# Batch 2's queries and keys turned by crossbar transposes from SyncE's queue, and two evictions split between VectorE and ScalarE, in a fused retention and expert kernel

## The chip, the cores and the metric

The kernel runs on one core of one Trainium2 chip. The metric is device time in microseconds (us): the median of three runs, 312.85 us before the change (312.38 to 313.4).

The engines by their short names: PE is TensorE (matmuls; PEld its weight loads), DVE is VectorE, ACT is ScalarE, POOL is GpSimd and SP is SyncE, which here only issues transfers. A transfer issued by SP waits in SP's queue, one issued by ScalarE in ScalarE's. "T" or "turn" below means: put a tile's 128 rows on its columns, so that PE can contract over the other dimension.

## What is computed

Retention over 8 batches of 8 heads, 576 positions and 64 dimensions, then a two-layer expert network on its result:

```python
scores = scale * np.matmul(q, k.transpose(0, 1, 3, 2))
Dmat = np.where(rel >= 0, gamma[:, None, None] ** rel[None, :, :], 0.0)
ret = np.matmul(scores * Dmat, v)             # per head; rel = row - column
x = ret.transpose(0, 2, 1, 3).reshape(B * S, H * D)      # 4608 x 512
h = x @ w_in                                             # 4608 x 2048
out = (h * sigmoid(beta * h)) @ w_out                    # 4608 x 512
```

Inputs and output are in f32; the kernel's matmuls take bf16 and add in f32.

## The kernel before

**The work.** Of each batch's 576 positions, 512 make four chunks of 128; the 64 left over (the tails) are taken in pairs of batches. Chunks are numbered through: 0 to 3 are batch 0, 4 to 7 batch 1, 8 to 11 batch 2. Since the decay is a power of the distance, it is put into the queries (`gq`) and the values (`gv`), and what remains is causal attention without softmax. For a chunk, `a_sc` (L312) multiplies turned keys `kT` with turned queries `qT` into scores `sc`, VectorE masks them into `R` (L332), `a_O` (L353) multiplies `R` with the values, `a_cross` (L334) adds what earlier chunks of the batch have left in a state, `a_x` (L370) copies the result out of PSUM into `xT`, and `a_st` (L383) adds the chunk to the state, which ScalarE copies to SBUF (`sbd`, or `end` after the last chunk; L398). The network runs on blocks of 512 rows: `up` (L403) makes one of 16 column groups of `h` and ScalarE applies the gate (L412); `down` (L416) makes one of four row groups of the output in four steps, VectorE copies it out (L430) and SP stores it (L433).

**How queries and keys are prepared.** SP loads them (`load_q` L80, `load_kv` L93). POOL (VectorE for batches 0 and 1) scales the queries into `qs` (L246); POOL casts the keys into `kn` (L272) and scales the values into `vn` (L254). Then they are turned in one of two ways. For batches below `XB = 3`, PE does it: `t_q` (L292) has two groups of eight transposes (L296) into a PSUM tile, copied to `qT` by ScalarE for one group and VectorE for the other (L297); `t_k` (L299) has four (L302), copied to `kT` by ScalarE (L303). From batch 3 on, and for the tails, `turn` (L279) has a crossbar transpose do it, SBUF to SBUF, issued from ScalarE's queue (L280): two for the queries of a batch (`x_q`), one for the keys of two chunks (`x_k`).

**The order.** It is written out by hand. `fill` is the list of network steps in the order in which PE takes them; a step (a unit) is one `up` or a quarter of one row group of a `down`. `d0` is the place where block 0's downs begin, `u1` where block 1's ups begin; `base[1]` is `u1 + 10`. The first twenty ups of block 1 are halves (two chunks of columns each), since its later chunks come late. Steps of the attention, of the loads and of the preparation have a place in `fill` as their due time, and `merged` (L440) puts them out by it, so that each engine's instructions, SP's and ScalarE's queues among them, stand in the order of these due times. An engine takes its instructions in this order; one that waits holds up all behind it.

`pair_steps` (L544) gives the due times of two chunks: `first` (state, scores of both) at `at`, `second` (products with the values, the cross terms, the copies to `xT`) at `to = at + 5`. For batch 2 the first pair's `at` is `lo = base[1] + 11` (L568). The second pair's is `hi`, eight units before block 2 begins.

Batch 1's chunks 4 to 7 have their own list (L530 to L536). Their copies to `xT` are made by ScalarE for even chunks and VectorE for odd ones (L381); chunk 3 alone is split, two pairs of heads on each engine (L378, L379). PE's halves of `up` on block 1 need `xT` of chunks 4 and 5 first, of 6 and 7 ten units later.

A transfer carries one of eight semaphores in turn, and waits for the transfer that had it last, eight issues before.

Of the kernel before, what the change touches and what calls it, by code (L numbers as in the profile page):

```python
# [19 lines left out]
def kernel(  # L20
# [10 lines left out]
    nc = tc.nc  # L31
# [9 lines left out]
    CB = MB // P  # L41
# [25 lines left out]

    NQ = 6
    E = CB
    XB = 3  # L70
    q_tiles, kv_tiles = {}, {}

    def load_q(b):
# [151 lines left out]
    def xt(m):  # L225
        if m not in xts:
            xts[m] = xpool.tile([P, HP, CB, P], BF16, name="xT", tag="xT" if m < B else "xTt", bufs=3 if m < B else 1)
        return xts[m]

    state_ps = {}  # L230
    batch, pair, live = {}, {}, {}
# [44 lines left out]
    def heads(t, p):  # L276
        return t[:, 2 * p:2 * p + 2, :].rearrange("p h d -> p (h d)")

    def turn(dst, src):  # L279
        nc.scalar.dma_start_transpose(dst.rearrange("p j pr s -> p (j pr) s"), src.rearrange("p j h d -> p (j h d)"))  # L280

    def x_q(b, u):
        turn(batch[b]["qT"][:, 2 * u:2 * u + 2], batch[b]["qs"][:, 2 * u:2 * u + 2])

    def x_k(b, u):
        kn, kT = pair[b, u]
        turn(kT, kn)

    def x_tail(i):
        turn(live[i]["qkT"], live[i]["qk"])  # L290

    def t_q(b, u):  # L292
        T = psum.tile([P, CB, 2, P], BF16, name="T", tag="mm" if u else "O", bufs=3 if u else 2)
# [5 lines left out]
    def t_k(i):  # L299
        T = psum.tile([P, HP, P], BF16, name="T", tag="sc" if i in (CB + 2, CB + 3) else "O", bufs=2)  # L300
        for p in range(HP):
            nc.tensor.transpose(T[:, p, :], heads(live[i]["kn"], p), ident[:])  # L302
        nc.scalar.copy(live[i]["kT"], T[:])  # L303

    def q_cols(i, r, p):

# [46 lines left out]
    def a_O(i):  # L353

        b, c = seq[i]
        L = live[i]

        early = i < E
        if not early:
            L["O"] = psum.tile([P, HP, P], F32, name="O", tag="O", bufs=2)  # L360
        O, R, vn = L["O"], L["R"], L["vn"]
        crossed = b is None or c > 0
        for j, p in [(n // HP, n % HP) if early else (n % 2, n // 2) for n in range(H)]:
            nc.tensor.matmul(O[j * D:(j + 1) * D, p, :], vn[:, 2 * p + j, :], R[:, j, p, :],  # L364
                             start=p == 0 and not (early and crossed), stop=early or not crossed,
                             skip_group_check=True)
        if early:
            a_x(i)

    def a_x(i):  # L370
        b, c = seq[i]
        O = live[i]["O"]
        if b is None:
            x = xt(B)[:, :, c, :]
        else:
            x, O = xt(b)[:, :, :, c * PC:(c + 1) * PC], O.rearrange("k p (i s) -> k p i s", i=CB)
        if i == CB - 1:
            nc.vector.tensor_copy(x[:, :2], O[:, :2])  # L378
            nc.scalar.copy(x[:, 2:], O[:, 2:])  # L379
        else:  # L380
            (nc.scalar.copy if i < E or i < 2 * E and i % 2 == 0 else nc.vector.tensor_copy)(x, O[:])  # L381

    def a_st(i):  # L383

# [65 lines left out]
    def F(f, *a):  # L450
        return lambda: f(*a)
# [9 lines left out]
    t_q(0, 1)  # L461
    pre(0)
    t_k(0)
    warm_up(2, 128)
    a_sc(0)
    a_st(0)
    pre(1)
    t_k(1)
    warm_up(1, 128)
    a_cross(0, True)  # L470
    a_O(0)
    a_sc(1)
    a_cross(1, True)
    pre(2, (0,))
    t_k(2)
    a_st(1)
    a_O(1)
# [28 lines left out]
    u1 = len(fill)  # L506
# [3 lines left out]
    base = {1: u1 + 10}  # L510
# [7 lines left out]
    def second(i):  # L518
        for f in (a_O, lambda j: a_cross(j, False), a_x):
            f(i)  # L520
            f(i + 1)
        a_st(i + 1)
# [21 lines left out]
    def pair_steps(i, at, to):  # L544
        b, c = seq[i]
        st = [(at, F(first, i)), (to, F(second, i))]
        if b is None:
            return st + [(at - 31, F(load_tail, c)), (at - 21.5, F(pre, i)), (at - 21, F(load_tail, c + 1)),
                         (at - 13, F(pre, i + 1)), (at - 12, F(x_tail, i)), (at - 9.5, F(x_tail, i + 1))]
        n = full.index(i)  # L550
        if b < XB:
            if c == 0:
                st += [(at - 12 + x, F(pre_q, b, x)) for x in range(4)]
                st += [(at - 5.5, F(t_q, b, 0)), (at - 4.5, F(t_q, b, 1))]
                st += [(at - 6.5 + x / 2, F(pre, i + x)) for x in range(CB)]
            return st + [(at - 3.5, F(t_k, i)), (at - 2.5, F(t_k, i + 1))]
        if c == 0:
            st += [(at - 30, F(load_q, b))] + [(at - 20 + x, F(pre_q, b, x)) for x in range(4)]
            st += [(at - 14 + 1.5 * x, F(x_q, b, x)) for x in range(2)]
        return st + [(at - 28, F(load_kv, n)), (at - 26, F(load_kv, n + 1)), (at - 16, F(pre, i)),  # L560
                     (at - 15, F(pre, i + 1)), (at - 10.5, F(x_k, b, c // 2))]

    todo = list(range(2 * CB, len(seq), 2))
    for n in range(1, B - 1):

        take = [i for i in todo if seq[i][0] == n + 1 or n == B - 2 or seq[i] == (None, 0) and n == CB - 1]
        todo = todo[len(take):]
        lo, hi = (base[n] + 11, base[n + 1] - 8) if n == 1 else (base[n] + 3, base[n + 1] - 8)  # L568
        if len(take) == 2 and n > 1:
            hi -= 6  # L570
        for x, i in enumerate(take):
            at = lo + x * (hi - lo) / (len(take) - 1)
            streams.append(pair_steps(i, at, at + 5))
# [32 lines left out]
```

## Time and profile before

| | |
|---|---|
| median of the runs | 312.85 us (312.38 to 313.4) |
| span of the profiled execution | 310.4 us |
| what lies around the span, against the median | 2.45 us |
| instructions in the span | 5341 |
| PE busy | 299.4 us |
| ScalarE, VectorE, POOL busy | 141.5, 110.1, 96.4 us |
| moved by DMA | 52.79 MB, mean 170 GB/s |
| crossbar transposes | 24, all on ScalarE's queue |
| granted TensorE clock, mean | 1.000 |

The profile is of one execution. Its time in the same measure as the runs is not recorded apart from the span, so the span and the 2.45 us stand for it. Times in views are microseconds from the start of the span. A row of a timeline has the start, the length of the stretch from its first instruction's start to its last one's end, the engine (SPq and ACTq are the issues of transfers), the line, the operation, the tiles as out<-in and the count. A row of the chain has the start, the time that counts towards the end, and what it went to. The time from a transfer's issue to its landing is given apart from these.

### The profile page before, as it was taken

Reading aid. Unit: us, or ns where it says so; the run is one execution under the profiler, and the core shown is the slowest. Engines: PE = TensorE matmul, PEld = TensorE weight load, DVE = VectorE, ACT = ScalarE, POOL = GpSimd, SP = SyncE. Lnnn points to the kernel's source line nnn. Section 1 sums busy time; section 2 is a strip of 40 time slices with the busy share of each in tenths; the row PEclk is TensorE's granted clock in tenths of the full one; section 3 lists DMA queues with packets and bytes.
Section 4 is the critical chain, followed back from the end, with each engine's and each line's share of the span. In section 5 each row is a group of like instructions: output and inputs, shape, how many; then the busy total and the mean of one; then the engine's idle time right before and its main releaser. Section 6 shows DMA issues by size and latency. Waiting matters only on the chain.

```text
span 310.4 us, 5341 instructions
## 1 busy us (share of the span) xinstructions
PE 299.4 (96%) x2142; PEld 157.3 (51%) x2177; DVE 110.1 (35%) x196; ACT 141.5 (46%) x250; POOL 96.4 (31%) x131
## 2 busy tenths in 40 slices
PE   7789999999999999999999999999999999999996
PEld 5544456765454454445544544545455454444444
DVE  6554476342433142434431434133415420010012
ACT  5577626984147502661077106720574037206700
POOL 4663026846524281362228021912420000000000
PEclk9999999999999999999999999999999999999999
DMA  7999999999979989996989598949832110041011
GB/s 202 220 354 386 380 239 269 234 233 200 234 163 170 215 183 230 230 204 98 243 228 112 120 211 224 194 100 208 195 60 50 68 70 0 9 93 37 0 67 71
DMA packets 123897, 52.79 MB, mean 170 GB/s; under 512 B 105680, under 2 KB 116320, under 8 KB 123872
## 3 DMA queue, kind: packets, MB, share of 16 engines
q1 hardware_dynamic: 98496, 46.15, 61.3%
q10 hardware_dynamic: 25376, 6.30, 13.5%
q8 instruction: 17, 0.28, 0.4%
q14 instruction: 8, 0.07, 0.1%
HBM read 36.71 MB, written 9.44 MB: 149 GB/s over the span
## 4 chain that ended last, share of the span: by engine, by line
PE 89%; SPq 4%; DMA 3%; issue 1%; DVE 1%; ACT 0%
PE po L423 40%; PE ph L410 38%; DMA wt<-in_moe_w_in_dram 3%; SPq L93 3%; PE O L364 3%; PE sc L322 3%; PE O L350 2%; PE st L393 2%; SPq L177 1%; PE T L296 1%; PE T L302 1%; DVE xT L381 0%; DVE w_in_sb L185 0%; PE O L347 0%; SPq L80 0%
## 5 line engine op out<-in xcount | busy, mean ns | idle before, releaser
L412 ACT ACTIVATE gT<-ph,beta_sb 128x512 bf16<-128x512 f32 (+1 forms) x154 | 100.4, 659 | 83.1 <-PE ph L410 82.4
L410 PE MATMUL ph<-xT,w_in_sb 128*128 128x512 bf16 (+1 forms) x599 | 128.9, 365 | 2.5 <-DVE w_in_sb L185 1.1
L423 PE MATMUL po<-w_out_sb,gT 128*128 128x512 bf16 (+2 forms) x590 | 127.4, 368 | 1.3 <-issue 0.5
L410 PEld LDWEIGHTS <-w_in_sb 128*128 128x128 bf16 x616 | 58.7, 98 | 64.3 <-DVE w_in_sb L185 2.2
L423 PEld LDWEIGHTS <-gT 128*128 128x128 bf16 x608 | 57.0, 98 | 62.3
L332 DVE TENSOR_TENSOR R<-sc,causal 128x512 bf16<-128x512 f32 x71 | 44.3, 684 | 56.5 <-PE sc L322 55.0
L430 DVE COPY ot<-po 128x512 f32<-128x512 f32 (+2 forms) x38 | 25.0, 662 | 86.2 <-PE po L423 83.4
L254 POOL TENSOR_TENSOR vn<-kvn,gv 128x512 bf16<-128x512 f32 x32 | 33.3, 1042 | 16.8 <-DMA kvn<-in_v_dram 15.5
L272 POOL CAST kn<-kvn 128x512 bf16<-128x512 f32 x32 | 19.6, 612 | 58.9 <-DMA kvn<-in_k_dram 58.5
L246 POOL TENSOR_TENSOR qs<-qn,gq 128x512 bf16<-128x512 f32 x24 | 24.3, 1042 | 27.3 <-DMA qn<-in_q_dram 27.3
L381 DVE CAST xT<-O 128x512 bf16<-128x512 f32 x30 | 19.4, 687 | 34.8 <-PE O L350 15.5
L398 ACT CAST sbd<-st 64x256 bf16<-64x256 f32 x48 | 17.5, 364 | 18.8 <-PE st L393 16.6
L398 ACT CAST end<-st 64x256 bf16<-64x256 f32 x16 | 5.9, 366 | 29.4 <-PE st L393 29.3
L393 PE MATMUL st<-vn,kn 128*128 128x128 bf16 x128 | 12.4, 220 | 0.2 <-POOL vn L254 0.2
L364 PEld LDWEIGHTS <-vn 128*64 128x64 bf16 x288 | 8.7, 110 | 6.7 <-issue 6.1
L364 PE MATMUL O<-R,vn 128*64 128x128 bf16 x288 | 11.9, 223 | 0.0
L303 ACT COPY kT<-T 128x512 bf16<-128x512 bf16 x12 | 6.9, 586 | 8.8 <-PE T L302 7.7
L393 PEld LDWEIGHTS <-kn 128*128 128x128 bf16 x128 | 9.0, 98 | 3.5
L322 PE MATMUL sc<-qT,kT 64*128 64x128 bf16 x256 | 10.3, 218 | 0.4 <-ACT kT L303 0.2
L322 PEld LDWEIGHTS <-kT 64*128 64x128 bf16 x288 | 8.1, 94 | 3.8 <-ACT kT L303 1.5
L350 PE MATMUL O<-qT,sbd 128*128 128x128 bf16 x96 | 8.3, 221 | 0.3 <-ACT xT L381 0.2
L207 PE MATMUL ph<-warm 128*128 128x128 f32 (+1 forms) x24 | 6.9, 426 | 1.2 <-DVE warm L118 1.2
(56 smaller groups left out, 85.8 us busy)
## 6 DMA issues: line engine op xcount, KB each, us to landing
qn<-in_q_dram SPq DMA_DIRECT2D x16, 512.0 KB, 5.5
kvn<-in_k_dram SPq DMA_DIRECT2D x32, 256.0 KB, 5.9
kvn<-in_v_dram SPq DMA_DIRECT2D x32, 256.0 KB, 5.7
out_dram<-ot SPq DMA_DIRECT2D x31, 256.0 KB, 2.8
wt<-in_moe_w_out_dram SPq DMA_DIRECT2D x4, 1024.0 KB, 9.5
wt<-in_moe_w_in_dram SPq DMA_DIRECT2D x4, 512.0 KB, 7.3
wt<-in_moe_w_in_dram SPq DMA_DIRECT2D x2, 1024.0 KB, 11.7
out_dram<-ot SPq DMA_DIRECT2D x9, 128.0 KB, 2.4
```

The lines of the kernel that those rows point to most:

```text
L246: e.tensor_tensor(batch[b]["qs"][:, cs, hs], q_tiles[b][:, hs, cs].rearrange("p h i d -> p i h d"), gq[:, cs, hs].unsqueeze(3).to_broadcas ...
L254: nc.gpsimd.tensor_tensor(live[i]["vn"][:], kv_tiles.pop(i)[:, 1], gains(gv, c), ALU.mult)
L272: nc.gpsimd.tensor_copy(kn[:, c % 2], t[:, 0])
L322: nc.tensor.matmul(view(sc[j][:, p, :]), L["kT"][r, p, :], rhs, start=True, stop=True, skip_group_check=True)
L332: nc.vector.tensor_tensor(R[:, j], sc[j][:], causal4[:] if i == CB - 1 else m_b, ALU.mult)
L364: nc.tensor.matmul(O[j * D:(j + 1) * D, p, :], vn[:, 2 * p + j, :], R[:, j, p, :], start=p == 0 and not (early and crossed), stop=early or ...
L393: nc.tensor.matmul(st[:, p, :], heads(L["kn"], p), heads(L["vn"], p), start=(c == 0 and p == 0), stop=True, skip_group_check=True)
L398: nc.scalar.copy(s[r, :, j * D:(j + 1) * D], st[r, :, j * D:(j + 1) * D])
L410: nc.tensor.matmul(ph, w_in_sb[:, ko, fo * P:(fo + 1) * P], xts[m][:, ko, :, w], start=(ko == 0), stop=(ko == KO - 1))
L412: nc.scalar.activation(gts[m][:, fo, :, w], ph, ACT.Silu, scale=beta_sb[:, fo:fo + 1])
L423: nc.tensor.matmul(po[:, :nn], gT[:, fo, ms, :], w_out_sb[:, fo, n0:n0 + nn], start=(fo == 0), stop=(fo == FO - 1))
L430: nc.vector.tensor_copy(ot, po[:, :nn])
```

## The change

- `XB` becomes 2 and is no longer a bound but one batch, the third (batch 2): its queries and keys are turned by crossbar transposes from SP's queue. Later batches and the tails keep theirs on ScalarE's. `t_q` and `t_k` are left to batches 0 and 1.
- Batch 2's preparation gets due times counted from `u1`; on POOL the order of instructions stays as it was. On SP the transposes of the queries (two) and of the first pair's keys stand behind block 0's four stores and ahead of the loads of batch 3's queries and its first two chunks; that of the second pair's keys stands behind these loads.
- Batch 2's first pair is due at `base[1] + 14` for `base[1] + 11`.
- The copies to `xT` of chunks 5 and 7 are split as chunk 3's is. ScalarE keeps chunks 4 and 6.
- The copy of chunk 7's turned keys goes from ScalarE to VectorE.

```diff
-    XB = 3
+    XB = 2
...
-    def turn(dst, src):
-        nc.scalar.dma_start_transpose(dst.rearrange("p j pr s -> p (j pr) s"), src.rearrange("p j h d -> p (j h d)"))
+    def turn(b, dst, src):
+        (nc.sync if b == XB else nc.scalar).dma_start_transpose(dst.rearrange("p j pr s -> p (j pr) s"), src.rearrange("p j h d -> p (j h d)"))
...
     def x_tail(i):
-        turn(live[i]["qkT"], live[i]["qk"])
+        turn(None, live[i]["qkT"], live[i]["qk"])
...
-        nc.scalar.copy(live[i]["kT"], T[:])
+        (nc.vector.tensor_copy if i == 2 * CB - 1 else nc.scalar.copy)(live[i]["kT"], T[:])
...
-        if i == CB - 1:
+        if i < 2 * CB and i % 2 and i != 1:
             nc.vector.tensor_copy(x[:, :2], O[:, :2])
             nc.scalar.copy(x[:, 2:], O[:, 2:])
         else:
-            (nc.scalar.copy if i < E or i < 2 * E and i % 2 == 0 else nc.vector.tensor_copy)(x, O[:])
+            (nc.scalar.copy if i < E or i < 2 * E else nc.vector.tensor_copy)(x, O[:])
...
-        if b < XB:
+        if b == XB:
             if c == 0:
-                st += [(at - 12 + x, F(pre_q, b, x)) for x in range(4)]
-                st += [(at - 5.5, F(t_q, b, 0)), (at - 4.5, F(t_q, b, 1))]
-                st += [(at - 6.5 + x / 2, F(pre, i + x)) for x in range(CB)]
-            return st + [(at - 3.5, F(t_k, i)), (at - 2.5, F(t_k, i + 1))]
+                st += [(u1 + 2 + x, F(pre_q, b, x)) for x in range(4)]
+                st += [(u1 + 6.5 + x / 2, F(pre, i + x)) for x in range(2)]
+                st += [(u1 + 9.5 + x / 2, F(pre, i + 2 + x)) for x in range(2)]
+                st += [(u1 + 10.1 + x / 10, F(x_q, b, x)) for x in range(2)]
+            return st + [(u1 + (12.1 if c == 0 else 20.1), F(x_k, b, c // 2))]
...
-        lo, hi = (base[n] + 11, base[n + 1] - 8) if n == 1 else (base[n] + 3, base[n + 1] - 8)
+        lo, hi = (base[n] + 14, base[n + 1] - 8) if n == 1 else (base[n] + 3, base[n + 1] - 8)
```

## The prediction

> **What bounds the kernel now.** I read the page's first two parts, then the chain of work that ended last, then the timelines of PE and of SP's queue around 60 to 80 us, where the change falls. From the page (busy time; 40 slices; DMA queues):
>
> ```profile
> PE 299.4 (96%) x2142; PEld 157.3 (51%) x2177; DVE 110.1 (35%) x196; ACT 141.5 (46%) x250; POOL 96.4 (31%) x131
> ...
> DMA  7999999999979989996989598949832110041011
> ...
> q1 hardware_dynamic: 98496, 46.15, 61.3%
> q10 hardware_dynamic: 25376, 6.30, 13.5%
> ```
>
> PE is the bound: what takes a microsecond off PE takes it off the end, and a microsecond in which PE waits is added. The second thing to see is the row of nines under DMA up to slice 11 (85 us): while batch 2 is fetched and prepared, the transfer engines are full. q1 is SP's queue, q10 ScalarE's, which carries the 24 crossbar transposes of later batches.
>
> The chain, in order of time (start us, us, what), around the steps that go:
>
> ```profile
> 62.28 0.45 PE T L296 x8
> ...
> 64.04 0.22 PE T L302 x4
> ...
> 66.32 0.22 PE st L393 x4
> 66.54 0.55 PE sc L322 x16
> ...
> 76.96 0.22 PE T L302 x4
> ...
> 80.22 0.55 PE sc L322 x16
> ```
>
> L296 and L302 are the transposes of queries and keys on PE; the sc at 66.54 belongs to batch 2's first pair of chunks (8 and 9), that at 80.22 to its second (10 and 11).
>
> **What goes.** Two groups of eight query transposes (0.45 us each) and four of four key transposes (0.22 each), all in the chain: 2 x 0.45 + 4 x 0.22 = 1.78 us of PE. Of these 1.34 stand before 66.54 and 0.44 behind it. Their copies out of PSUM go too (ScalarE 1.01 and 4 x 0.59 us, VectorE 0.69), off the path: at most 0.3 us, since PE has gaps of 0.1 to 0.3 us while ScalarE is full from 62 to 66 us.
>
> **What is moved.** The first pair's products are put three units later (base + 14 for base + 11). Each unit is four matmuls of 128x512, 0.865 us by the chain's 4.42 us for 20. That is an exchange of order and costs nothing by itself. Without a wait, the sc of chunks 8 and 9 would come at 66.54 - 1.34 + 2.60 = 67.8 us. It now waits for two query transposes and one key transpose from SP's queue.
>
> **When they land.** In the changed program SP issues in the same order as before up to the last two stores of block 0 (L433); then come the three transposes, then the loads of batch 3 (two of queries, four of keys and values), then the second pair's transpose. So SP reaches them when it now reaches L80. SP's timeline (start, us, what):
>
> ```profile
> 61.00 1.02 SPq L93 DMA_DIRECT2D kvn<-in_v_dram  x1
> 62.12 3.78 SPq L433 DMA_DIRECT2D out_dram<-ot  x2
> 65.95 1.04 SPq L80 DMA_DIRECT2D qn<-in_q_dram  x2
> ```
>
> Those two stores need blocks that VectorE had written by 51.2 us; SP is late because the queue is full, not for want of data, and nothing in the change lightens the queue ahead of them. The operands of the transposes are ready earlier: POOL ends chunk 9's keys at 61.4 us, in an order that is unchanged. So the first transpose is issued at 65.95. What one costs, by two of ScalarE's at 204 us, when the transfer engines were nearly idle (one tile's instructions in a window; duration min/median/max in ns):
>
> ```profile
> L280 ACTq DMA_TRANSPOSE qT<-qs x2: 1249/1274/1298, 204.5 to 205.8; - x2
> DMA to landing us min/median/max: 3.2/3.2/3.2
> ```
>
> No row shows a transpose on SP's queue, so I bound the landing of the third (the keys). Early end: 65.95 + 2 x 1.27 + 3.2 = 71.7. Late end: they stand in line behind the last store (issued 65.07, 4.1 to landing: 69.2), each taking 1.75 us: q10 held 13.5% of 310.4 us for 24. That gives 69.2 + 3 x 1.75 = 74.4. At 1.3 us each, the issue pace, it is 73.1. I take 72.4, between the issue-bound 71.7 and this 73.1, since rows at 117 to 119 us move 224 GB/s with transposes nearly alone, 1.2 us for one.
>
> Advanced Engine Details and Errata, section X-Bar Transpose (TRN2), in the Trainium skill holds transposes to be as fast as plain transfers. Here the queue totals give 150 GB/s against 243 for q1, though in the stretch named they come near. By the page the line would move at q1's 1.08 us for 256 KB, and the keys would land at 72.4 as well.
>
> **The sum.** Products start at 72.5 instead of 67.8: PE idles 4.7 us. Against before the end moves by 72.5 - 66.54 - 2.60 (three units already done) - 0.44 (transposes no longer to come) = **+2.9 us** (bounds +2.2 and +4.9). The break-even landing is 69.5 us. Nothing later gives it back: from 67 us on the chain is PE to the end, with no wait over about 0.6 us.
>
> **PE's clock after the gap.** The longest idle time of PE in this profile is about 0.6 us, so no row shows what 4.7 us do. The trace's clock records give the nearest rows: full clock is granted from 4.9 us, 3.7 us after the first matmul (1.25), and half again at 312.1, 4.8 us after the last one ends (307.35). A drop would cost up to half of such a 3.7 us stretch, 1.85 us; no drop costs 0. The gap is within 0.1 us of the row's 4.8, so I take the middle, **+0.9**.
>
> TensorE: Matmul & The Clock Gate, Part 1, in the Trainium skill says that an idle window of about 3.4 us brings half clock, on a grid that does not start with the kernel; the two records are 90 such windows apart, which agrees. By it 1.7 us would be added for one window, in those executions whose grid lies so.
>
> **The eviction splits and the moved copy.** Chunks 5 and 7 go half by VectorE, half by ScalarE. In the one such split now, the waits list ScalarE's half as waiting for VectorE's (L379 for L378, 0.7 us): they run one after the other, 425 + 372 ns and 34 between, 0.83 us against 0.69 whole. But two of PE's four next matmuls need only the first half, so PE's first group ends some 0.08 us sooner: 0.15 for both places. Chunk 7's key copy goes from ScalarE (0.59) to VectorE, between a half of its 691 ns for 128x1024 and 0.59, in 1.5 us of its idle time. All this lies ahead of 67.8, so the wait swallows it; it counts only if there is no wait.
>
> **Behind the transposes.** The batch 3 loads queue behind them, some 3.3 to 5 us later. Their products start at 91.94 now, keys landed at 87.5: 4.4 us of room, and PE itself is 2.9 later. ScalarE's transposes for batch 3 wait until the second pair's has landed. That one lands at 72.4 + 8.0 (what the six loads took from 69.2 to 77.2) + 1.3 to 1.75 = 81.7 to 82.2; PE asks for it at 80.22 + 2.9 = 83.1. So it is hidden.
>
> Own time: span 310.4 plus 2.45 around it is the median of the runs shown, 312.85. With +2.9 and +0.9: **316.7 us**.
>
> **Rivals.**
> 1. *The transposes land in time* (the other side). Mechanism: SP gets past the stores early, and the 1.78 + 0.15 us come off: **310.9**. It decides from a landing at 69.5, that is SP at the transposes by 69.5 - 5.7 = 63.8 or sooner; fully only at 67.8, SP at 62.1. For it: the stores' bare issue is 0.36 us each and they take 3.78, so a stretch of 3 us could shrink. Against: the same DMAs are ahead, on full engines. 0.12. Partly so, within 0.3%: 0.06.
> 2. *The second pair decides.* If SP's issue behind the first three is stretched (now one load there takes 3.2 us), the second pair's keys land after 83.1, and ScalarE's copies of the state, queued behind its waiting transposes, are late for the product at 85.76 + 2.9. At a landing of 86 the shift is 86 - 80.2 = 5.8: **318.7**. Against: 82 by the sum above. 0.10.
> 3. *The forecast* with its unknowns: 0.72, from 315.0 (71.7, no drop) to 319.6 (74.4 and a drop).
>
> The range, 313.9 to 319.7, holds the forecast's bounds, most of rival 2 and a little of an earlier SP; rival 1 is left out. About 0.3% is what a measurement can tell from no change: slower 0.82, same 0.06, faster 0.12.
>
> **What would show it.** In the changed profile: three L280 on SPq from about 66 us on; in the waits PE's L322 (or its weight load) waiting some 4.7 us for a DMA of kT or qT; an idle PE in slices 9 to 10; perhaps a PEclk digit below 9 after it; no L296 or L302 after 60 us. It would be wrong if SP issues the first transpose before 63.8, or if the keys land within 3 us of a late issue.

## The result, and the profile after

| | before | after |
|---|---|---|
| median of 6 runs each, us | 312.81 (312.38 to 315.01) | **317.38** (314.93 to 319.54) |
| ratio after / before | | **1.0136** [1.0107, 1.0166], slower by 1.4% |
| span of the profiled execution, us | 310.4 | 312.7 |
| that execution's own time, us | | 314.93 |
| mean granted TensorE clock in it | 1.000 | 0.999 |
| crossbar transposes on SP's queue / on ScalarE's | 0 / 24 | 4 / 24 |

The ratios in this document and their intervals are the record's estimates over all runs of a group. They are not the quotients of the medians, which here is 1.0146.

The runs of after are far apart. Each, with the mean clock that PE was granted in it: 314.93 (0.999), 316.17 (0.995), 316.95 (0.995), 317.80 (0.994), 318.21 (0.993), 319.54 (0.988). The profiled execution is the quickest of them, and the only one that kept its clock. So its trace shows the wait alone, and the clock has to be read from other traces below.

From the page of after, the answer to the page of before (busy time; 40 slices of 7.8 us; DMA queues):

```profile
PE 298.2 (95%) x2110; PEld 155.6 (50%) x2145; DVE 109.2 (35%) x196; ACT 138.1 (44%) x246; POOL 96.3 (31%) x131
...
PE   7789999968999999999999999999999999999996
...
PEclk9999999999999999999999999999999999999999
DMA  8999999999999799995998495949943110041012
...
q1 hardware_dynamic: 102720, 47.20, 63.4%
q10 hardware_dynamic: 25376, 6.30, 15.2%
```

PE is still the bound and has a microsecond less to do, but its ninth and tenth slices (62.5 to 78.2 us) are down to 6 and 8 tenths. q1 carries 1.05 MB more, and the DMA row is still full from its second slice to its thirteenth.

SP's timeline of after, answering to the three lines of before (start, us, what):

```profile
60.90 0.94 SPq L93 DMA_DIRECT2D kvn<-in_v_dram  x1
61.94 2.51 SPq L433 DMA_DIRECT2D out_dram<-ot  x2
64.61 3.40 SPq L280 DMA_TRANSPOSE qT<-qs  x2
68.11 1.28 SPq L280 DMA_TRANSPOSE kT<-kn  x1
69.44 1.15 SPq L80 DMA_DIRECT2D qn<-in_q_dram  x2
...
76.78 2.24 SPq L280 DMA_TRANSPOSE kT<-kn  x1
```

The transposes stand behind block 0's last two stores and ahead of batch 3's loads. SP came to them at 64.61; L80, which had this place before, came at 65.95.

The chain that ended last, around the same steps (start, the time that counts, what):

```profile
60.90 5.39 DMA kvn<-in_v_dram
...
67.50 0.50 SPq L280
...
68.11 3.16 DMA kT<-kn
71.27 0.05 issue
71.32 0.62 PE sc L322 x16
...
81.80 0.22 PE st L393 x4
82.02 0.55 PE sc L322 x16
```

L296 and L302 are gone from it. In their place it leaves PE for a load of values, SP's issues of the transposes (the piece at 67.50 is the end of the second query transpose's) and the transfer of the keys. The step from the load to SP is the profile's inference: the queries and keys that are turned here were ready by 61.2 us. The keys land at 71.27, 3.16 us after their issue, and the first pair's scores start 0.05 later. PE's timeline (idle time and its releaser in brackets), and PE's waits (us in total, times, longest):

```profile
67.47 0.39 PE L393 MATMUL st<-vn,kn 128*128 128x128 bf16 x4
71.32 0.62 PE L322 MATMUL sc<-qT,kT 64*128 64x128 bf16 x16 [3.46 <-DMA kT<-kn]
```

```profile
PE sc L322 <- DMA kT<-kn: 3.5, 1, 3.5
```

This is the longest wait in PE's list. Without it the scores would have come at 71.32 - 3.46 = 67.86. Against before PE is 1.80 us late at the second pair's scores (82.02 for 80.22), 1.96 at 107 us and 2.31 from 135 us to its end (309.65 for 307.35). The second pair does not wait: its keys landed at 81.40, 0.62 us before PE asked.

### The profile page after: what moved, and what is told of

Same layout as the page of the kernel before. It is cut to its first block, busy times and chain, and to the rows that moved or that the text cites. A ratio compares the mean times of both kernels' runs of the same rounds, so it can differ in the third digit from the quotient of the medians.

```text
span 312.7 us, 5282 instructions
## 1 busy us (share of the span) xinstructions
PE 298.2 (95%) x2110; PEld 155.6 (50%) x2145; DVE 109.2 (35%) x196; ACT 138.1 (44%) x246; POOL 96.3 (31%) x131
## 4 chain that ended last, share of the span: by engine, by line
PE 75%; SPq 11%; DMA 9%; POOL 2%; issue 1%; DVE 1%; ACT 0%; POOLq 0%
PE po L423 35%; PE ph L410 31%; SPq L93 8%; DMA wt<-in_moe_w_in_dram 4%; PE O L364 3%; PE sc L322 2%; DMA qn<-in_q_dram 2%; DMA kvn<-in_v_dram 2%; PE O L350 2%; PE st L393 2%; SPq L80 1%; POOL qs L246 1%; SPq L177 1%; DMA kT<-kn 1%; POOL vn L254 1%
## 5 line engine op out<-in xcount | busy, mean ns | idle before, releaser
L412 ACT ACTIVATE gT<-ph,beta_sb 128x512 bf16<-128x512 f32 (+1 forms) x154 | 99.6, 659 | 87.9 <-PE ph L410 87.3
L272 POOL CAST kn<-kvn 128x512 bf16<-128x512 f32 x32 | 19.6, 612 | 59.4 <-DMA kvn<-in_k_dram 59.2
L381 DVE CAST xT<-O 128x512 bf16<-128x512 f32 x28 | 18.0, 686 | 32.2 <-PE O L364 15.2
L261 POOL TENSOR_TENSOR kn<-tln,gq 128x512 bf16<-128x512 f32 x4 | 4.2, 1042 | 11.8 <-DMA tln<-in_q_dram 7.7
```

The source lines that it names most:

```text
L412: nc.scalar.activation(gts[m][:, fo, :, w], ph, ACT.Silu, scale=beta_sb[:, fo:fo + 1])
```

## The experiments

The theory was: the wait for the turned keys is the loss, it comes from the place of the transposes in SP's queue behind two stores, and most runs lose clock on top. Rivals: the splits cost something; a transfer later in the program would take back what the transposes save, even without the wait; transposes on this stretch of full transfer engines do not pay on any queue. The kernel before was run beside each group of them: 313.08 for e1 to e4, 312.47 for e5 to e8, 312.85 for e9 to e11, 313.07 for e12.

| kernel | median, us | ratio to before |
|---|---|---|
| e1, before + splits and moved copy | 313.98 | 1.002 [1.0, 1.0041] |
| e2, after without the first wait | 321.26 | 1.0258 [1.0222, 1.0293] |
| e3, after, first pair four units later | 320.99 | 1.0243 [1.0209, 1.0277] |
| e4, after, PE kept busy in the wait | 318.51 | 1.017 [1.0129, 1.021] |
| e5, after, second key transpose early | 318.64 | 1.0156 [1.0114, 1.0197] |
| e6, e5 without the first wait | 312.54 | 0.9993 [0.9979, 1.0008] |
| e7, e5, PE kept busy in the wait | 314.81 | 1.0067 [1.0047, 1.0088] |
| e8, e5, stores behind the transposes | 312.61 | 0.9999 [0.9982, 1.0017] |
| e9, e6, stores behind batch 3's loads | 311.26 | 0.9953 [0.9935, 0.997] |
| e10, e5, stores behind batch 3's loads, first pair two units later | **311.00** | **0.9942** [0.9923, 0.996] |
| e11, after, all transposes on ScalarE's queue | 321.24 | 1.0254 [1.0227, 1.0281] |
| e12, before, stores behind batch 3's loads | 312.75 | 0.9997 [0.9984, 1.001] |

### e1: the splits alone

The kernel before, with the edits of the change to L303, L377 and L381 and nothing else:

```diff
-        nc.scalar.copy(live[i]["kT"], T[:])
+        (nc.vector.tensor_copy if i == 2 * CB - 1 else nc.scalar.copy)(live[i]["kT"], T[:])
...
-        if i == CB - 1:
+        if i < 2 * CB and i % 2 and i != 1:
...
```

> The kernel before, with only the two split evictions (chunks 5 and 7) and chunk 7's key copy on VectorE; batch 2 is still turned on PE. Theory (the loss is all in the wait for the crossbar transposes): the splits are worth 0.08 us each, so 312.7 us, not to be told from before. Rival (two engines one after the other cost 0.14 us more per chunk, and the copy moved to VectorE delays the masks): 313.1 to 313.5, and PE's wait ahead of its next up grows.

Measured 313.98 against 313.08: 0.2% slower by the ratio, with an interval that ends at 1.0. The splits bring no gain; a small cost, which the rival expected, is not excluded. In the profiled execution PE is 0.4 us late at the scores of chunks 8 and 9 already, and waits 0.79 us at 128 us for a gate of ScalarE (L412), far from the edit. Which part of the 0.2% is the edit's own, the record does not show.

### e2: no wait for the first pair

```diff
+        kT = live[i - 4]["kT"] if i in (2 * CB, 2 * CB + 1) else L["kT"]
...
-                rhs, view = q_cols(i, r, p)
+                rhs, view = q_cols(i - 4 if i in (2 * CB, 2 * CB + 1) else i, r, p)
...
```

> The changed kernel, whose scores of chunks 8 and 9 alone use batch 1's turned queries and keys (of chunks 4 and 5), which are there long before: the scores of these two chunks are left out in favour of wrong ones of the same size. All transposes are still made, on the same queue; only the wait ahead of the first pair's scores is gone. Theory: the time falls to the time before less 1.8 to 1.9, about 311.0 us, and the runs lie within 0.5 us of each other, clock 1.00. Rival (the three transposes cost by their share of the transfer engines, or by pushing batch 3's loads back): above 312.5.

The kernel leaves out the right scores of chunks 8 and 9. The theory was missed, and the rival's bound (above 312.5) passed for another reason: 321.26. The first wait is gone, and a longer one stands at the second pair. SP's waits list, then SP's, ScalarE's and PE's timelines of e2 (an added line moves the later line numbers up by one in e2, e6 and e9, and by nine where the stores are collected; L419 is then the store):

```profile
SPq L280 <- DMA qT<-qs: 6.5, 2, 4.8
```

```profile
75.19 1.02 SPq L93 DMA_DIRECT2D kvn<-in_v_dram  x1
82.83 1.25 SPq L280 DMA_TRANSPOSE kT<-kn  x1
```

```profile
77.71 3.25 ACTq L280 DMA_TRANSPOSE qT<-qs  x2
```

```profile
78.01 0.39 PE L394 MATMUL st<-vn,kn 128*128 128x128 bf16 x4
85.96 1.04 PE L323 MATMUL sc<-qT,kT 64*128 64x128 bf16 x16 [7.57 <-DMA kT<-kn]
```

In after, ScalarE's first transpose for batch 3 waits for SP's second key transpose (81.56, after a landing at 81.40). In e2 it is the other way round: SP sits from 76.2 to 82.83 until ScalarE's two query transposes have landed, and PE sits 7.57 us behind that. The built program lets only one of the two transposing queues go at a time, and the edit, which touches neither, changed which goes first. SP's wait stands in its own instructions, and all six runs lie between 320.72 and 322.08. The run says nothing on the first wait; it says what this order is worth. The cure is to have the second key transpose issued well ahead (e5).

### e3: the first pair four units later

```diff
-        lo, hi = (base[n] + 14, base[n + 1] - 8)
+        lo, hi = (base[n] + 18, base[n + 1] - 8)
```

> The changed kernel with the first pair of batch 2 due at base + 18 for base + 14: four units, 3.5 us, more of the network ahead of it. Theory: the wait falls from 3.5 us or more to 0 to 2, too short for the clock to drop; 311.2 to 313 us, runs close together. Rival (the second pair or ScalarE's later transposes set the end): stays above 315, with the wait at another place.

The theory was missed and the rival right: 320.99. The first wait shrinks from 3.46 to 0.54 us, as expected; then PE waits 3.41 us ahead of the state at 81.85 and 3.56 for `kT` at 86.00, with the order of the queues turned round as in e2. The profile puts the 3.41 us down to POOL's keys (L272, done at 81.76), but those are batch 3's. By the times PE was held up by ScalarE's copy of the state, on which it waits too and which ran from 80.97 to 81.71, behind the two query transposes that held ScalarE's queue from 77.68 to 80.92.

### e4: PE kept busy in the wait

Twelve matmuls of 128x512 whose results nothing reads, ahead of the first pair's scores:

```diff
+    def busy(n):
+        ph = psum.tile([P, MB], F32, name="ph", tag="mm", bufs=3)
+        for _ in range(n):
+            nc.tensor.matmul(ph[:], w_in_sb[:, 0, :P], w_in_sb[:, 0, :MB], start=True, stop=True,
...
         a_st(i)
+        if i == 2 * CB:
+            busy(12)
```

> The changed kernel with twelve matmuls of 128x512 whose result nobody reads (2.6 us) on PE right ahead of the first pair's scores, where it would idle. The keys land as before. Theory of the clock (in most executions the idle time lowers the granted clock for some microseconds): the idle time left is 1 to 3 us, the clock stays at 1.00 and the median falls by 1.5 to 2.5 us, to 315 to 316, though PE does more work. Rival (the executions differ only in when the keys land): median and spread stay, 316.5 to 318.

318.51, inconclusive: the queues are turned round here too. But its trace shows how little idle time takes the clock away. PE's timeline of e4:

```profile
81.58 0.39 PE L393 MATMUL st<-vn,kn 128*128 128x128 bf16 x4
84.19 0.62 PE L322 MATMUL sc<-qT,kT 64*128 64x128 bf16 x16 [2.22 <-DMA kT<-kn]
84.75 6.18 PE L423 MATMUL po<-w_out_sb,gT 128*128 128x512 bf16 x20
```

PE idles 2.22 us, and the same twenty matmuls that took 4.48 us at 77.27 take 6.18. The clock records give half clock from 85.57 to 88.98.

### e5: the second key transpose early

```diff
-            return st + [(u1 + (12.1 if c == 0 else 20.1), F(x_k, b, c // 2))]
+            return st + [(u1 + (12.1 if c == 0 else 14.9), F(x_k, b, c // 2))]
```

> The changed kernel with one due time moved: the second pair's key transpose at u1 + 14.9 for u1 + 20.1, which puts it on SP's queue right behind the first three and ahead of batch 3's loads. Of itself it should change nothing, since that transpose was in time: 316 to 318.5 us, the wait for the first pair's keys 3.5 us or more as in the changed kernel, no other wait. It is the base for the next three, in which the second pair's keys can then not come late behind ScalarE's transposes, as they did in the versions without a first wait (7.6 us), with the later due time (3.6) and with the extra matmuls (2.2). Rival (the place of that transpose matters): below 315.

318.64, just above the 316 to 318.5 that the theory expected and far from the rival's 315. It is after with the order of the two queues made safe, and so the base for what follows. Its profiled execution has what that of after lacks, a lost clock. The PEclk row of its page, and PE's timeline:

```profile
PEclk9999999995999999999999999999999999999999
```

```profile
67.45 0.39 PE L393 MATMUL st<-vn,kn 128*128 128x128 bf16 x4
72.78 1.03 PE L322 MATMUL sc<-qT,kT 64*128 64x128 bf16 x16 [4.94 <-DMA kT<-kn]
73.74 3.60 PE L410 MATMUL ph<-xT,w_in_sb 128*128 128x512 bf16 x8
```

SP came to the transposes at 66.67 here, the keys landed at 72.73, and PE idled 4.94 us. The clock is half from 71.45 to 78.28: the sixteen score matmuls take 1.03 us for 0.62, eight of the network's 3.60 for 1.89. Of that stretch PE works 5.5 us, so 2.75 are lost. The six runs show the same two kinds: 315.39 at a mean clock of 0.998, and 316.66 to 319.83 at 0.993 to 0.989.

### e6: e5 without the first wait

e5 with the edit of e2.

> The same, and the scores of chunks 8 and 9 use batch 1's turned queries and keys, as in the version without a wait: the right scores of these two chunks are left out. No wait should be left on PE. Theory (the waits are the whole loss): the time before less 1.8, about 311.0 us, clock 1.00, runs within 0.7 us. Rival (the transposes cost beside the wait): above 312.5.

312.54, level with before, where the theory said 311.0. The wait and its clock are the whole loss (318.64 to 312.54), but the 1.8 us that the missing transposes save is not there either: the rival's outcome. PE is 1.85 us ahead at 78 us, 1.49 at 90, 0.82 at 106 and from there to the end. PE's timeline and ScalarE's at these two places:

```profile
90.38 0.62 PE L323 MATMUL sc<-qT,kT 64*128 64x128 bf16 x16 [0.29 <-DMA kT<-kn]
...
99.65 4.48 PE L411 MATMUL ph<-xT,w_in_sb 128*128 128x512 bf16 x19 [0.51 <-ACT gT L413]
```

```profile
95.53 2.58 ACTq L280 DMA_TRANSPOSE kT<-kn  x1
98.14 0.74 ACT L399 CAST sbd<-st 64x256 bf16<-64x256 f32 x2 [1.99 <-POOL kn L262]
```

The last of batch 3's first six loads landed 5.45 us later than before (82.63 for 77.18), its keys are turned late, and PE, now early, waits for them. Then ScalarE stands in the issue of a transpose, the copy of the state behind it is late, and so is the next gate. That is 1.0 us of 1.8 in this execution.

### e7: e5, PE kept busy in the wait

e5 with the edit of e4.

> The same base with twelve matmuls of 128x512 that nobody reads (2.6 us) ahead of the first pair's scores, where PE idles. Theory of the clock: idle time falls to 1 to 2 us, the clock stays at 1.00, and the median comes down by 1.5 to 2.5 us against the base, to about 315, with runs closer together. Rival (no part of the clock): median as the base's, within 0.5.

314.81, by the medians 3.8 us quicker than e5 (2.8 by the ratios) with 2.75 us more work on PE, and all runs but one between 314.63 and 315.22. The clock is 1.000 in the profiled execution and 0.998 or more in every run. This is more than the 1.5 to 2.5 expected. Not all of it need be the clock: in the profiled execution the keys landed 1.25 us earlier than in e5's (71.49 for 72.73). PE is 2.23 us late at the end, nearly what after showed with its clock kept (2.31).

### e8: block 0's stores behind the transposes

e5, with the four stores of block 0 collected and issued by SP after the first three transposes:

```diff
...
-            nc.sync.dma_start(rows[:, ms, n0:n0 + nn], ot)
+            if m == 0:
+                held.append((rows[:, ms, n0:n0 + nn], ot))
+            else:
+                store(rows[:, ms, n0:n0 + nn], ot)
...
-    streams = [[(0, F(load_w_out, 0)),
+    streams = [[(u1 + 12.2, F(late_stores))], [(0, F(load_w_out, 0)),
```

> The same base with block 0's four stores issued behind the four transposes' first three instead of ahead of them; nothing else is changed. Theory (SP's place behind the stores sets the landing): SP issues the first transpose at about 61.5 us for 64.6, the keys land near 67.5 to 68.5, PE waits 0 to 0.7 us; 311.0 to 312.0 us, below the kernel before. Rival (the transfer engines are full anyway, and the place in the queue changes little): a wait of over 2 us stays, above 314.

312.61: 6.0 us quicker than e5 by the medians (4.9 by the ratios), level with before, a little over the 311 to 312 expected. SP's timeline of e8:

```profile
60.93 3.41 SPq L280 DMA_TRANSPOSE qT<-qs  x2
64.45 1.91 SPq L280 DMA_TRANSPOSE kT<-kn  x1
66.45 2.16 SPq L419 DMA_DIRECT2D out_dram<-ot  x4
```

The transposes go 5.7 us earlier than in e5, the keys land at 68.44 for 72.73, and PE waits 0.74. It is 1.03 us ahead of before at the second pair and 0.73 at the end. From SP's first transpose to the landing it is 7.51 us here and 6.06 in e5, so the gain is SP's earlier arrival, not quicker transfers. So the loss is the place in the queue, not the transposes.

### e9 and e10: the stores behind batch 3's loads

e9 is e6 with the stores held until `u1 + 20.2`, behind batch 3's loads. e10 is e5 with that, and with the first pair two units later:

```diff
-        lo, hi = (base[n] + 14, base[n + 1] - 8)
+        lo, hi = (base[n] + 16, base[n + 1] - 8)
...
-    streams = [[(0, F(load_w_out, 0)),
+    streams = [[(u1 + 20.2, F(late_stores))], [(0, F(load_w_out, 0)),
```

> The version without a wait and with early keys (scores of chunks 8 and 9 from batch 1's turned queries and keys, so the right ones of these chunks are left out), and block 0's four stores issued behind batch 3's loads (due u1 + 20.2). Theory (the 1.8 us that PE saves are given back because the four transposes push batch 3's loads 3 us back, so that its keys and ScalarE's work behind their transposes are late at 90 and 99 us): batch 3's loads land as early as before the change, no wait over 0.3 us is left after 60 us, and the time is 310.8 to 311.6. Rival (the gain goes elsewhere): 312.3 to 312.8, as without the move.

> The changed kernel as it should compute, with early keys, block 0's four stores behind batch 3's loads, and the first pair due at base + 16. Theory: SP issues the transposes from 61 us on, the keys land at 68 to 68.5 us, PE asks at 69.5, no wait; batch 3's loads are not late: 310.8 to 311.8, below the kernel before by 0.3% or more. Rival (transfer engines remain too full for all that is due): 312.3 or more with a wait somewhere from 60 to 110 us.

e9 came to 311.26 and e10 to 311.00, both as expected; e10 is **0.6% quicker than before** (0.9942 [0.9923, 0.996]). SP's and PE's timelines of e10:

```profile
60.22 1.04 SPq L93 DMA_DIRECT2D kvn<-in_v_dram  x1
61.43 3.40 SPq L280 DMA_TRANSPOSE qT<-qs  x2
64.94 3.73 SPq L280 DMA_TRANSPOSE kT<-kn  x2
...
75.66 4.64 SPq L419 DMA_DIRECT2D out_dram<-ot  x5
```

```profile
63.83 5.45 PE L410 MATMUL ph<-xT,w_in_sb 128*128 128x256 bf16 x25
69.12 0.39 PE L393 MATMUL st<-vn,kn 128*128 128x128 bf16 x4
69.44 0.62 PE L322 MATMUL sc<-qT,kT 64*128 64x128 bf16 x16
```

The keys land at 69.22, later than the 68 to 68.5 expected; PE asks for them at 69.44 and waits for no transfer. The last of batch 3's first six loads lands at 79.40, for 82.63 in e6 and 77.18 before. In the profiled executions PE keeps 1.68 us (e9) and 1.28 (e10) to the end.

### e11: the transposes on ScalarE's queue

```diff
-        (nc.sync if b == XB else nc.scalar).dma_start_transpose(
+        nc.scalar.dma_start_transpose(
```

> The changed kernel with all transposes on ScalarE's queue again, one line undone; due times as in the change. Theory (it is SP's queue that delays the landing): the first pair's keys land by about 66 to 67 us, no wait at 67.8; but each issue holds ScalarE for 1.3 us or more among the gates of block 1, so PE waits for PSUM in pieces of 0.5 to 1.5 us: 312 to 314 us, no clock drop. Rival (full transfer engines delay it on any queue): keys after 70 us, a wait of over 2 us, above 315.

321.24: the theory was missed, and the rival right on the time and the landing, though PE's waits are for gates and not for the keys. ScalarE's and PE's timelines of e11:

```profile
61.38 3.67 ACTq L280 DMA_TRANSPOSE qT<-qs  x1
65.09 0.47 ACT L412 ACTIVATE gT<-ph,beta_sb 128x256 bf16<-128x256 f32 x1 [4.35 <-issue]
65.20 4.14 ACTq L280 DMA_TRANSPOSE kT<-kn  x1
...
69.39 1.20 ACT L412 ACTIVATE gT<-ph,beta_sb 128x256 bf16<-128x256 f32 x3 [3.46 <-issue]
```

```profile
65.62 1.86 PE L410 MATMUL ph<-xT,w_in_sb 128*128 128x256 bf16 x8 [4.15 <-ACT gT L412]
69.91 2.51 PE L410 MATMUL ph<-xT,w_in_sb 128*128 128x256 bf16 x11 [2.43 <-ACT gT L412]
```

With the transfer engines full, two issues hold ScalarE for 3.67 and 4.14 us; its gates queue behind, and PE waits for those, 4.15 and 2.43 us, before it comes to the scores. The clock is half from 65.52 to 75.76 us. The keys land no earlier (72.73), although the first transpose was issued at 59.77: 12.96 us to the landing, for 7.51 in e8. Why, is open. It was not for new transfers of SP's: after the load at 61.34 its next ones went at 68.98 and 72.74, when ScalarE's first transpose (68.91) and the keys (72.73) had landed and left them their semaphores. SP has nothing else to do while an issue is held; ScalarE has.

### e12: the stores alone

The kernel before with the stores held as in e10:

> The kernel before, with only block 0's four stores held back until batch 3's loads have been issued, as in e10_stores_last. It tells whether e10's 1.8 us come from the transposes or from the stores alone. Theory: PE in the kernel before waits for no transfer between 60 and 100 us (no wait over 0.6 us, and none for a DMA), so the order on SP alone moves nothing, and the transposes are what e10 gains: within 0.3% of the kernel before, 312.4 to 313.2 for a kernel before at 312.8. Rival: the earlier loads of batches 2 and 3 remove small waits by themselves, so that most of e10's gain is there without the transposes: below 311.8. Second rival: the held stores keep two more output tiles in use and VectorE waits for them: above 313.8.

312.75, level with before (0.9997 [0.9984, 1.001]), as the theory said. So e10's gain needs the transposes; the order of the stores only lets them be in time. The first pair's later place was not tried in the kernel before.

## Why the prediction was right, and where its sizes were off

The forecast's case happened: slower, by a wait for the keys behind two stores in SP's queue, with a loss of clock after it. The median, 317.38, lies 0.7 us over the 316.7 forecast. Step by step:

- **Where the products would come without a wait**: 67.8 predicted, 67.86 measured. (By the chain's 4.42 us for 20 matmuls three units are 2.65 us, not 2.60.)
- **SP at the transposes**: 65.95 predicted, 64.61 in after, and 63.9 (e3) to 66.7 (e5) over the seven executions that had the same transfers ahead (after, e2 to e7). One profile of before gave one draw of that; the 63.8 from which rival 1 decides was never quite reached.
- **From there to the landing**: 6.45 us predicted (72.4 - 65.95), 6.66 in after, and 6.06 (e5) to 7.47 (e3) over the seven. The two query issues took 3.50 us for 2.54, the last landing 3.16 for 3.2. The landings stand 0.96 and 1.15 us apart (69.16, 70.12, 71.27), so they pass a little quicker than the 1.2 and 1.3 of the working. The landing itself, 71.27, is below the stated bound of 71.7, as it is in six of the seven (71.20 to 71.59), since SP was early; e5's, 72.73, is within.
- **Idle time and shift**: 4.7 and +2.9 predicted; 3.46 and +1.80 in after at the second pair, +2.31 at the end. The wait was oversized by the late arrival of SP that the one profile of before showed; e5, whose SP came late too, has 4.94 us of idle time.
- **The clock**: +0.9 predicted, as the middle between no drop and half of a 3.7 us stretch. This term was mis-sized, by the chance above all: five runs of six had a drop. One 3.41 us window of half clock in 315 us makes a mean of 0.995, two make 0.989; so four of the five lost one window, worth at most 1.7 us, and one lost two. The median stands 2.45 us over the one run that kept its clock, so some 0.7 us of that is not the clock. What it is stays open; when the keys landed is known for the profiled run alone. In e5, where the drop lasted 6.8 us, the median stands 3.25 us over the run that kept its clock, and e7 puts at most 3.8 on it. The error here is the other way from that in the wait: 2.1 (314.93 against 312.81) and 2.45 for 2.9 and 0.9. They cancel in part, and that the sum came within 0.7 us is so far luck. (Before has one wait longer than the 0.6 us named: 1.2 us ahead of its first matmuls.)
- **The skill's clock rule**: TensorE: Matmul & The Clock Gate, Part 1, in the Trainium skill has the clock fall after one idle window or more of about 3.4 us. The grid agrees (the records of every trace here are whole multiples of 3.413 us apart), but e4's drop came after a window in which PE was idle for only 2.04 of 3.41 us. By the measurement less than a wholly idle window is enough.
- **The splits**: predicted 0.15, swallowed by the wait. e1 finds no gain when there is nothing to swallow it.
- **Behind the transposes**: the second pair was predicted to land 81.7 to 82.2 and to be hidden; it landed at 81.40 and was, by 0.62 us. e2, e3 and e4 show that this hung on one order of the two queues. In e3 PE waits for ScalarE's copy of the state behind its held transposes, which is part of rival 2's mechanism.
- **"Nothing later gives it back"** held for the changed kernel, where PE is late. Of the gain of rival 1, 310.9, it did not: with the wait gone and nothing else changed (e6) batch 3's later loads take back 1.0 us in the trace and all of the gain in the median. The room of 4.4 us before batch 3's products was counted against a PE that is late, not against one that is 1.8 us early. Only with the stores behind batch 3's loads too is rival 1's number met (e9 311.26, e10 311.00).

Open: how much of e5's distance to e7 is the clock and how much an earlier landing, and what the rest of the spread in after is. The run-to-run times were not resolved further than by each run's mean clock.

## What to carry to other kernels

When work moves from a busy engine to a transfer, ask first where in its queue the transfer stands: here the same four transposes cost 1.4% behind two stores that nobody waited for, and gained 0.6% with those stores behind the loads, the second key transpose early and the first pair two units later. A wait on the bounding engine costs more than its length if the engine's clock falls, and such a loss shows as a spread of the runs and of their granted clock, not in the one profile that kept it. Four transposes ahead of the loads, in a full stretch of transfers, pushed the last of batch 3's first six loads back by 5.45 us (e6), so the room of the next stage is to be counted for the case that the change succeeds.

## What the runs showed of the hardware

- **Part of a window is enough for the clock to fall.** The grid points follow from each trace's clock records. Windows in which PE idled 1.53 and 1.93 of 3.41 us (after) brought no drop; 2.04 us (e4) and 2.74 us (e3) did. At the programs' ends 1.82, 1.87 and 1.91 us brought none (e8, e10, e11), and 2.08 did (after). Half clock then lasted one window (e4, 3.4 us), two (e5 and e2, 6.8) or three (e3 and e11, 10.2): each time until the first window in which PE did not idle. Windows with 0.98 to 2.83 us of idle time in between kept half clock. The phase of the grid is another in each execution, so the same wait costs differently from run to run.
- **An issue of a transpose can be held where the transfer engines are full**: 1.25 to 1.3 us where they were nearly idle, and between that and 2.68 on SP (e3) or 4.14 on ScalarE (e11) where they were full. On ScalarE the engine's own work stands behind it.
- **Transposes on SP's queue** landed 3.1 to 5.9 us after their issue, and one behind another 0.8 to 1.4 us apart. On ScalarE's queue in e11 it was 7.0 to 9.2 us.
- **Two queues that transpose wait for each other.** In e2 SP's key transpose went at 82.83, after ScalarE's second query transpose had landed (82.76); in after ScalarE's went at 81.56, after SP's had landed (81.40). Which goes first is set by waits in the built program, and edits elsewhere turned it round: a wait of 7.57 us on PE in e2.
